# Fused attention, Sinkhorn gate and experts on one core: the first expert's weight loads put behind the transposes of five steps

## The chip, the cores and the metric

The kernel runs on one core of a Trainium2 chip. The metric is device time in microseconds (us). TensorE (PE) multiplies, VectorE (DVE) and ScalarE (ACT) work on tiles element by element, GpSimd (POOL) copies, and SyncE (SP) issues every DMA of this kernel from one queue.

## What is computed

The reference is attention with a bias learnt from relative positions, and behind it eight experts whose outputs are summed with weights from a Sinkhorn gate:

```python
def _attn_ref(q, k, v, w1, b1, w2):          # q, k, v: (4, 8, 576, 64)
    scores = scale * np.matmul(q, k.transpose(0, 1, 3, 2))
    ...
    h = np.maximum(x @ w1 + b1, 0.0)
    bias = h @ w2
    scores = scores + bias.transpose(2, 0, 1)[None, :, :, :]
    attn = np.exp(scores - np.max(scores, axis=-1, keepdims=True))
    attn = attn / (np.sum(attn, axis=-1, keepdims=True) + 1e-09)
    return np.matmul(attn, v)

def _moe_ref(x, w_gate, w1, w2):             # x: (2304, 512), 8 experts, F = 1024
    P = np.exp(logits - logits.max())        # then 8 Sinkhorn rounds on P
    for e in range(E):
        h = np.maximum(x @ w1[e], 0.0)
        out += P[:, e:e + 1] * (h @ w2[e])
```

Matrix products run as sums of three fp16 products: each fp32 operand is cut into a high and a low fp16 part.

## The kernel before

The kernel has two stages, each with a plan of its own. In the first, code records its instructions as nodes of a `Plan` (`record`, `node`), with the tile regions that each reads and writes; `Plan.emit` then runs a model of the engines with estimated durations and emits all nodes in the order in which the model starts them. So the order of every engine's instructions, and of SP's queue, comes from that model, and a dependency between nodes in the plan moves other nodes too. Waits between engines in the built program come from the tiles that instructions really touch. The plan holds SP's DMAs as an engine named "dma".

The attention part of stage one goes in steps (`steps`, `for n in range(NS + LAG + 1)`). A step treats one or two tiles of 128 queries of one head: PE makes scores `s`, DVE adds the bias and takes the minimum (`sb`), ACT takes the exponential, DVE the reciprocal (`st`), ACT and DVE write the high and low halves of the weights (`ah`, two buffers), and SP issues a DMA transpose of `ah` into `aT` (three buffers; `aT4` for single tiles). Two steps later PE multiplies `aT` with the values (`pv`), and the result goes to the expert input `xa`, `xb` or `xc`. Each unit of four tile pairs also loads `nat` (queries and keys), `vnat` (values) and `bt` (bias).

Beside the steps, `w_stage(j)`, called in step n = j + 6, brings in the weights of the first expert: `w_load(which, i)` issues one load of 512 KB (which = 0 is layer 1, which = 1 is layer 2, four loads each) into a part of `area`; `w_max` takes the largest absolute value of a load (a reduction on DVE, for two of the loads an activation on ACT); `w_scale` makes the scale of a layer from them; `w_cut` cuts a load into two fp16 halves (ACT and DVE). The places of the layer-1 loads 2 and 3 were used by the bias before, whose last results SP moves from `area` to `br`; those loads wait for these transfers. `e0_pieces` are pieces of expert 0's matmuls on PE (`l` tiles), put between the steps once weights and inputs are there.

The call that the change rewrites stands at L1061 to L1067 of the kernel before:

```python
if j == 0:
    for i in (2, 3):
        w_load(0, i)
    for i in (2, 3):
        w_max(0, i)
    for i in range(4):
        w_load(1, i)
```

Stage two (from the gate matmuls at L1264 on) computes the gate and all experts with a plan of its own.

Of the kernel before, what the change touches and what calls it, by code (L numbers as in the profile page):

```python
# [42 lines left out]
class Plan:  # L43
# [11 lines left out]
        ("pe", "dve"): 0.2,  # L55
    }

    def record(self, eng, cost, fn, ins, outs, move=None):
        g = self.group
        if g is not None:  # L60
            g[0] = eng
            g[1] += cost
            g[2].append(fn)
            for new, l in ((ins, g[3]), (outs, g[4])):
                l.extend(r for r in map(region, new) if r not in l)
            return
        self.node(eng, cost, fn, [region(x) for x in ins], [region(x) for x in outs], move)
# [40 lines left out]
        self.node(g[0], g[1], lambda: [f() for f in g[2]], g[3], g[4])  # L108

    def __init__(self):  # L110
        self.group, self.seen, self.prio = None, {}, 1
        self.nodes, self.writer, self.readers = [], {}, {}

    def add(self, eng, cost, fn, reads=(), writes=(), prio=1, after=0.0):
# [59 lines left out]
def region(ap):  # L174

    b = mybir.dt.size(ap.dtype)
    dims, off = list(ap.ap), ap.offset
    p = (0, 1)
    if ap.space != DRAM:
        step, n = dims.pop(0)  # L180
        p = (off // step, off // step + n)
        off %= step
    lo, hi = off * b, (off + sum((n - 1) * st for st, n in dims) + 1) * b
    if ap.space == PSUM:
        lo, hi = lo // 2048 * 2048, -(-hi // 2048) * 2048
    return ap.name, p, (lo, hi)
# [84 lines left out]
def attention_sinkhorn_moe(ctx, tc, q, k, v, w1, b1, w2, wg, m1, m2, xm, xm4, xf, sel, out):  # L271
# [11 lines left out]
    plan = Plan()  # L283
# [13 lines left out]
    def sm(shape):  # L297
        used[0] += shape[1]
        assert used[0] <= SMALL
        return sms[: shape[0], used[0] - shape[1] : used[0]]  # L300
# [100 lines left out]
    def w_src(e, which, i):  # L401
        if which == 0:
            return m1[e, i * P : (i + 1) * P, :]
        return m2[e, 2 * i * P : (2 * i + 2) * P, :].rearrange("(a p) d -> p a d", p=P)

    def w_dst(which, t):
        return t if which == 0 else t.rearrange("p (a d) -> p a d", a=2)
# [5 lines left out]
    with ExitStack() as actx:  # L413
# [375 lines left out]
        for n in range(8):  # L789
            for m in (2 * n, 2 * n + 1):  # L790
                nm, _, i = qk_order[m]
# [22 lines left out]
        g = sm([P, 1])  # L814
# [204 lines left out]
        def w_load(which, i):  # L1019
            raw[which, i] = f = wp[4 * which + i + 1]  # L1020
            sync.dma_start(out=w_dst(which, f), in_=w_src(0, which, i))

        def w_max(which, i):
            m, f = mw[:, 4 * which + i], raw[which, i]
            if (which, i) not in W_SUMS:
                absmax(m[:, 0:1], f)
                return
            for j in range(2):
                junk = wrk.tile([P, DM], F32, name="ys", tag="ys")
                act.activation(junk, f[:, 512 * j : 512 * j + 512], AF.Abs, accum_out=m[:, j : j + 1])  # L1030

        def w_scale(which):
            n = 2 - which
            m = sm([P, n])
            vec.tensor_reduce(
                out=m[:, 0:1], in_=mw[:, 4 * which : 4 * which + 4].rearrange("p n i -> p (n i)"), axis=AX.X, op=ALU.max
            )
            if which == 0:
                absmax(m[:, 1:2], wgt.rearrange("p a e -> p (a e)"))
            with plan.urgent():  # L1040
                u_, s_ = pow2(bcast_max(ps_small, m, n), n, TM14, TINY)
            wsc[which] = (u_[:, 0:1], s_[:, 0:1])
            if which == 0:
                wsc["ug"] = u_[:, 1:2]
                split(wgs[:, 0], wgs[:, 1], wgt, s_[:, 1:2])
            else:
                uw[0] = (wsc[0][0], wsc[1][0])

        def w_cut(which, i):
            w = wp[4 * which + i].bitcast(F16).rearrange("p (a n) -> p a n", a=2)  # L1050
            f, sc = raw.pop((which, i)), wsc[which][1]
            asplit(w[:, 0, :], w[:, 1, :], f, sc)
            (w1t if which == 0 else w2t).setdefault(0, {})[i] = w

        def w_stage(j):
            if j == -4:
                sync.dma_start(out=wgt, in_=wg.rearrange("(a p) e -> p a e", p=P))
            if j in (-4, -3):
                w_load(0, j + 4)
                w_max(0, j + 4)  # L1060
            if j == 0:  # L1061
                for i in (2, 3):
                    w_load(0, i)
                for i in (2, 3):
                    w_max(0, i)
                for i in range(4):
                    w_load(1, i)  # L1067
            if j == 5:
                w_scale(0)
                for i in range(4):  # L1070
                    w_cut(0, i)
            if j == 6:
                for i in range(4):
                    w_max(1, i)
                w_scale(1)
                for i in range(4):
                    w_cut(1, i)
# [7 lines left out]
        steps = []  # L1085
# [44 lines left out]
        W0 = 6  # L1130
        for n in range(NS + LAG + 1):
# [31 lines left out]
            if n == W0 - 1:  # L1163
                assert bpos[0] > NBLK
                hpl = Places(lambda k, n, size: area[:, 8192:])
            w_stage(n - W0)
            for _ in range(2 if n % 5 in (0, 2, 4) or n < 20 else 1):
                if pieces and n >= 13:
# [694 lines left out]
    for n, (e, b) in enumerate(seq):  # L1863
        r = visit[n]
        i, at_end, leaves = (b, r % 2), n % 5 == 4, visit[n + 1 : n + 2] != [r]
# [96 lines left out]
```

## Time and profile before

| what | us |
|---|---|
| median of 3 runs | 1778.55 |
| lowest and highest run | 1778.25, 1781.21 |
| profiled execution, its own time | 1782.07 |
| span of the profiled execution, first to last instruction | 1780.3 |
| PE, DVE, ACT busy in the span | 1682.0, 1448.0, 1087.9 |

The span is 1.8 us shorter than the time of the same execution; the rest lies around the instructions. The profiled execution took 3.5 us more than the median. Attention fills the span up to about 512 us, the gate and the rest of expert 0 some 70 us more, and the other experts what follows. All instructions of stage one are recorded by a helper and so carry its line, L210 (L217 in the changed kernel); they are told apart by their tiles.

### The profile page before, as it was taken

Reading aid. Unit: us, or ns where it says so; the run is one execution under the profiler, and the core shown is the slowest. Engines: PE = TensorE matmul, PEld = TensorE weight load, DVE = VectorE, ACT = ScalarE, POOL = GpSimd, SP = SyncE. Lnnn points to the kernel's source line nnn. Section 1 sums busy time; section 2 is a strip of 40 time slices with the busy share of each in tenths; the row PEclk is TensorE's granted clock in tenths of the full one; section 3 lists DMA queues with packets and bytes.
Section 4 is the critical chain, followed back from the end, with each engine's and each line's share of the span. In section 5 each row is a group of like instructions: output and inputs, shape, how many; then the busy total and the mean of one; then the engine's idle time right before and its main releaser. Section 6 shows DMA issues by size and latency. Waiting matters only on the chain.

```text
span 1780.3 us, 40365 instructions
## 1 busy us (share of the span) xinstructions
PE 1682.0 (94%) x16640; PEld 1374.5 (77%) x16640; DVE 1448.0 (81%) x2627; ACT 1087.9 (61%) x1930; POOL 79.9 (4%) x91
## 2 busy tenths in 40 slices
PE   7886897899989999999999999999999999999998
PEld 4554564555666788888988898889888988898887
DVE  6987989889967898778878787878788878876666
ACT  7886888788855675645564555564555544453443
POOL 0120112212200000000000000000000000000000
PEclk9988899999989999999999999999999999999999
DMA  7769999999893254645474556445655653463321
GB/s 256 246 160 223 207 210 204 188 205 194 190 281 117 85 197 179 231 156 173 170 276 135 196 198 241 155 149 212 209 177 179 240 187 131 163 237 102 104 73 36
DMA packets 294141, 323.70 MB, mean 182 GB/s; under 512 B 184252, under 2 KB 220612, under 8 KB 288964
## 3 DMA queue, kind: packets, MB, share of 16 engines
q1 hardware_dynamic: 293956, 321.12, 60.6%
q8 instruction: 130, 2.13, 0.5%
q14 instruction: 55, 0.45, 0.1%
HBM read 189.33 MB, written 88.08 MB: 156 GB/s over the span
## 4 chain that ended last, share of the span: by engine, by line
PE 83%; DVE 6%; DMA 5%; ACT 3%; issue 2%; SPq 0%; DVEq 0%; ACTq 0%
PE bankA L1585 18%; PE bankA L1605 14%; PE bankE L1585 9%; PE bankE L1605 9%; PE bankB L1605 9%; PE l L210 7%; PE bankB L1585 5%; PE s L210 4%; PE pv L210 3%; DMA aT<-ah 3%; ACT area L210 2%; PE bankA L393 2%; DVE area L210 1%; DVE ah L210 1%; DVE sb L210 1%
## 5 line engine op out<-in xcount | busy, mean ns | idle before, releaser
L1585 PEld LDWEIGHTS <-slot 128*128 128x128 f16 x5040 | 450.7, 98 | 49.9 <-issue 4.1
L1605 PEld LDWEIGHTS <-hA 128*128 128x128 f16 x2268 | 222.3, 98 | 27.3 <-issue 0.6
L210 PEld LDWEIGHTS <-area 128*128 128x128 f16 (+1 forms) x2477 | 153.6, 100 | 102.7 <-issue 35.0
L1585 PE MATMUL bankA<-xt,slot 128*128 128x256 f16 (+1 forms) x1680 | 186.1, 262 | 1.8 <-ACT u L1642 1.8
L1585 PE MATMUL bankE<-xt,slot 128*128 128x256 f16 (+1 forms) x1680 | 186.1, 262 | 0.0
L1630 ACT ACTIVATE hA<-c 128x512 f16<-128x512 f32 x189 | 118.2, 627 | 110.0 <-DVE c L1208 109.1
L1605 PEld LDWEIGHTS <-hS 128*128 128x128 f16 x1512 | 147.3, 98 | 21.7 <-ACT hS L1630 2.8
L1605 PEld LDWEIGHTS <-area 128*128 128x128 f16 x1512 | 147.9, 98 | 18.5 <-issue 1.4
L1208 DVE SCALAR_TENSOR_TENSOR hA<-c,hA 128x512 f16<-128x512 f32 x189 | 127.6, 686 | 14.2 <-ACT hA L1630 12.2
L210 DVE SCALAR_TENSOR_TENSOR ah<-sb,st,ah 128x576 f16<-128x576 f32 x144 | 120.6, 863 | 18.6 <-ACT ah L210 18.4
L1689 ACT COPY u<-bankA 128x512 f32<-128x512 f32 (+1 forms) x70 | 37.9, 542 | 158.8 <-PE bankA L1605 158.4
L210 ACT ACTIVATE ah<-sb,st 128x576 f16<-128x576 f32 x144 | 106.4, 772 | 34.2 <-DMA aT<-ah 29.6
L1642 ACT ACTIVATE u<-bankA 128x512 f32<-128x512 f32 x126 | 75.2, 597 | 68.1 <-PE bankA L1585 63.9
L210 PE MATMUL l<-area 128*128 128x512 f16 (+1 forms) x413 | 110.8, 385 | 4.9 <-ACT area L210 1.5
L210 ACT ACTIVATE sb<-sb,st 128x576 f32<-128x576 f32 x144 | 110.5, 769 | 7.9 <-DVE st L210 7.4
L1208 DVE SCALAR_TENSOR_TENSOR acc<-c,fs,acc 128x256 f32<-128x256 f32 x252 | 110.7, 481 | 2.0
L210 PE MATMUL s<-qkT 128*128 128x512 f16 (+3 forms) x560 | 83.5, 301 | 21.9 <-DVE st L210 21.0
L1605 PE MATMUL bankA<-area,hS 128*128 128x256 f16 x756 | 88.6, 273 | 2.9 <-ACT hS L1630 2.2
L1605 PE MATMUL bankA<-area,hA 128*128 128x256 f16 x756 | 89.9, 276 | 0.0
L1605 PE MATMUL bankA<-area 128*128 128x256 f16 x756 | 88.2, 273 | 1.0 <-ACT u L1689 1.0
L1605 PE MATMUL bankE<-area,hS 128*128 128x256 f16 x756 | 88.3, 273 | 0.0
L1605 PE MATMUL bankB<-area,hA 128*128 128x256 f16 x756 | 88.2, 273 | 0.0
(240 smaller groups left out, 3155.0 us busy)
## 6 DMA issues: line engine op xcount, KB each, us to landing
sc_w<-stage SPq DMA_DIRECT2D x84, 512.0 KB
acc<-sc_y SPq DMA_DIRECT2D x102, 256.0 KB
area<-sc_w SPq DMA_DIRECT2D x48, 512.0 KB
sc_y<-acc SPq DMA_DIRECT2D x84, 256.0 KB
xt<-sc_t SPq DMA_DIRECT2D x18, 1024.0 KB
slot<-sc_w SPq DMA_DIRECT2D x36, 512.0 KB
bt<-sc_bias SPq DMA_DIRECT2D x26, 576.0 KB
raw<-in_moe_w_dram SPq DMA_DIRECT2D x28, 512.0 KB
```

Of the source, the lines that this page charges most:

```text
L210: self.plan.record(self.name, cost, lambda: fn(*args, **kw), ins, outs, move)
L393: pe.matmul(ps[:, :512], h[a][:, ft, j * P : (j + 1) * P], w[:, wl, c : c + 512], start=(ft == 0 and i == 0), stop=(ft == 7 and i == 2),)
L1208: vec.scalar_tensor_tensor(out=o, in0=x, scalar=s, in1=y, op0=op0, op1=op1)
L1585: pe.matmul(ps[:, jf * w : jf * w + w], t[:, a, c * 512 + f * P : c * 512 + f * P + P], x(xp, c), start=(first and jf == 0 and c == 0 and ...
L1605: pe.matmul(ps[:, j * 256 : j * 256 + 256], h[:, a, fc * w + j * P : fc * w + j * P + P], t[:, wp, fc * 256 : fc * 256 + 256], start=(firs ...
L1630: on_act(0.58, lambda: act.activation(h[:, 0, sl], x, AF.Relu if relu else AF.Copy), [r], wk)
L1642: on_act(0.55, lambda: act.activation(tmp[k], bank[b], f, scale=HS), [b], [k], 0)
L1689: on_act(0.27 * nt, lambda: act.copy(tmp[k][:, :n], bank[b][:, :n]), [b], [k], 0)
```

## The change

`Plan` gets a context manager `behind`: while it is open, each recorded node also counts the given tiles as inputs. With it the loads of `w_stage` are put behind the transpose of a step, in the plan alone:

```diff
+    @contextmanager
+    def behind(self, *aps):
+
+        self.also = list(aps)
+        yield
+        self.also = []
+
     def record(self, eng, cost, fn, ins, outs, move=None):
-        g = self.group
+        g, ins = self.group, [*ins, *self.also]
...
-            if j == 0:
-                for i in (2, 3):
-                    w_load(0, i)
+            if 0 <= j < 5:
+                with plan.behind(steps[j + W0 - 1]["aT"]):
+                    for i in (2, 3) if j == 0 else (j - 1,):
+                        w_load(int(j > 0), i)
+            if j == 2:
                 for i in (2, 3):
                     w_max(0, i)
-                for i in range(4):
-                    w_load(1, i)
```

(`W0` is 6, the first step behind the bias.) The layer-1 loads 2 and 3 stay in step 6, the four layer-2 loads go to steps 7 to 10, and the reductions of the layer-1 loads 2 and 3 are recorded in step 8. The numbers of instructions of PE, ACT and POOL stay the same, and so do those of the loads.

SP's queue from the last two value loads before the weight loads on, in the kernel before (`moe_w` are the weight loads; 128x1024 is layer 1, 128x2x512 layer 2; x2 is two in a row):

```order
L210 DMA vnat_116<-in_v_dram 64x2x256
L210 DMA area<-in_moe_w_dram 128x2x512
L210 DMA br_111<-area 64x4x128 x2
L210 DMA_TRANSPOSE aT_123<-ah_144 128x18x128
L210 DMA br_111<-area 64x4x32 x2
L210 DMA area<-in_moe_w_dram 128x1024
L210 DMA br_111<-area 64x4x32 x2
L210 DMA area<-in_moe_w_dram 128x2x512 x2
L210 DMA area<-in_moe_w_dram 128x1024
L210 DMA area<-in_moe_w_dram 128x2x512
L210 DMA_TRANSPOSE aT_125<-ah_142 128x18x128
L210 DMA_TRANSPOSE aT_138<-ah_144 128x18x128
```

The first weight load stood ahead of the transpose into aT_123, and five stood between that one and the next two. From here on the same place in the changed kernel, up to the second layer-2 load:

```order
L217 DMA_TRANSPOSE aT_123<-ah_144 128x18x128
L217 DMA br_111<-area 64x4x128 x2
L217 DMA nat_128<-in_k_dram 128x576
L217 DMA nat_120<-in_q_dram 128x576
L217 DMA br_111<-area 64x4x32 x2
L217 DMA area<-in_moe_w_dram 128x1024
L217 DMA br_111<-area 64x4x32 x2
L217 DMA_TRANSPOSE aT_125<-ah_142 128x18x128
L217 DMA area<-in_moe_w_dram 128x1024
L217 DMA_TRANSPOSE aT_138<-ah_144 128x18x128
L217 DMA area<-in_moe_w_dram 128x2x512
L217 DMA bt_122<-sc_bias 128x1152
```

The transpose into aT_123 now comes first, one layer-1 load stands before that into aT_125 and one behind it, and two `nat` loads have moved in ahead of them. Behind these rows the queue goes on so:

```order
L217 DMA area<-in_moe_w_dram 128x2x512
L217 DMA_TRANSPOSE aT_123<-ah_142 128x18x128
L217 DMA bt_124<-sc_bias 128x1152
L217 DMA area<-in_moe_w_dram 128x2x512
L217 DMA_TRANSPOSE aT_125<-ah_144 128x18x128
L217 DMA_TRANSPOSE aT_0_118<-ah_142 128x9x128
L217 DMA bt_122<-sc_bias 128x1152
L217 DMA area<-in_moe_w_dram 128x2x512
L217 DMA_TRANSPOSE aT_138<-ah_144 128x18x128
```

The layer-2 loads stand between the next transposes, the second one directly behind a `bt` load. On DVE, before, the reductions of the loads (`TENSOR_REDUCE sms<-area`) stood together:

```order
L210 TENSOR_REDUCE sms<-area 128x1
L210 TENSOR_SCALAR st_132<-st_132 128x1
L210 RECIPROCAL st_132<-st_132 128x1
L210 TENSOR_REDUCE sms<-area 128x1 x2
L210 TENSOR_REDUCE sms<-sms 128x1
L210 TENSOR_REDUCE sms<-l_0_114 2x1
L210 TENSOR_SCALAR sms<-ident,sms 2x2
L210 TENSOR_REDUCE sms<-area 128x1
```

Now two of them stand between the cuts of layer 1 (`area<-area`) and the work of the steps (`ISA sb` adds the bias and takes the minimum), and the two others further on:

```order
L217 SCALAR_TENSOR_TENSOR area<-area,sms 128x1024
L217 TENSOR_REDUCE sms<-area 128x1
L217 TENSOR_SCALAR st_135<-st_135 128x2
L217 TENSOR_REDUCE sms<-area 128x1
L217 SCALAR_TENSOR_TENSOR ah_142<-sb_136,st_132,ah_142 128x576
L217 SCALAR_TENSOR_TENSOR area<-area,sms 128x1024
L217 ISA sb_141,st_139<-s_117,bt_124,sms 128x576
```

The work of the steps that stood behind all reductions now stands among them. The order of all engines differs from here to the end of the attention part, in patches that grow smaller.

## Rows read from the trace of the kernel before

**Rows 1.** The page: the chain that ended last, by engine.
```profile
PE 83%; DVE 6%; DMA 5%; ACT 3%; issue 2%; SPq 0%; DVEq 0%; ACTq 0%
```

**Rows 2.** Timeline of PE (start us, us, engine, line, operation): the first gate matmuls.
```profile
512.46 1.36 PE L1264 MATMUL bankS<-wgs,xa 128*128 128x8 f16 x48
```

**Rows 3.** Busy time by stretch: length, each engine's us (instructions), clock, DMA share, GB/s.
```profile
core 0: us, PE busy (x) PEld busy (x) DVE busy (x) ACT busy (x) POOL busy (x), PEclk, DMA share, GB/s
150.00:160.00 10.00, 5.85 (x62) 3.28 (x59) 9.96 (x24) 7.33 (x16) 0.00 (x0) 0.98 1.11 258
160.00:190.00 30.00, 17.30 (x102) 9.21 (x101) 22.85 (x56) 15.46 (x31) 0.00 (x0) 0.56 1.01 232
190.00:210.00 20.00, 16.03 (x164) 10.68 (x164) 19.62 (x40) 19.13 (x33) 1.63 (x3) 0.91 0.96 230
210.00:250.00 40.00, 39.21 (x408) 25.40 (x409) 36.83 (x83) 33.12 (x68) 7.58 (x7) 1.00 0.94 182
250.00:300.00 50.00, 42.53 (x411) 26.52 (x410) 44.90 (x98) 42.23 (x86) 9.29 (x10) 0.93 1.02 215
```

**Rows 4.** The chain of waits, 165 to 186 us: start us, us, what.
```profile
165.39 3.00 DMA br<-area
...
168.54 0.86 DMA area<-in_moe_w_dram
169.40 8.70 DMA aT<-ah
178.13 1.44 ACT ah L210 x2
...
185.65 2.09 PE s L210 x8
```

**Rows 5.** Timeline of SP's queue, 154 to 179 us.
```profile
154.01 0.53 SPq L210 DMA_DIRECT2D area<-in_moe_w_dram  x1
...
157.16 5.12 SPq L210 DMA_TRANSPOSE aT<-ah  x1
...
164.16 0.54 SPq L210 DMA_DIRECT2D area<-in_moe_w_dram  x1
...
166.05 3.31 SPq L210 DMA_DIRECT2D area<-in_moe_w_dram  x4
169.40 9.55 SPq L210 DMA_TRANSPOSE aT<-ah  x2
```

**Rows 6.** Timelines of DVE (two rows of `ah`, one reduction) and ACT.
```profile
159.71 0.82 DVE L210 SCALAR_TENSOR_TENSOR ah<-sb,st,ah 128x576 f16<-128x576 f32 x1
...
165.31 1.55 DVE L210 SCALAR_TENSOR_TENSOR ah<-sb,st,ah 128x576 f16<-128x576 f32 x2 [1.96 <-ACT ah L210]
...
172.10 1.22 DVE L210 TENSOR_REDUCE sms<-area 128x1 f32<-128x1024 f32 x1 [2.13 <-DMA area<-in_moe_w_dram]
...
178.13 1.44 ACT L210 ACTIVATE ah<-sb,st 128x576 f16<-128x576 f32 x2 [6.94 <-DMA aT<-ah]
```

**Rows 7.** Timeline of SP's queue, 194 to 201 us.
```profile
194.84 0.42 SPq L210 DMA_DIRECT2D nat<-in_k_dram  x1
196.17 3.62 SPq L210 DMA_TRANSPOSE aT<-ah  x1
...
200.47 0.42 SPq L210 DMA_DIRECT2D nat<-in_q_dram  x1
```

**Rows 8.** DMA engines, 40 slices: 150:160, 160:180 (and GB/s), 180:200, 250:270, 270:290.
```profile
DMA  9986899999977798999999999999999999999999
...
DMA  9932999553768998998989569999998699999999
GB/s 141 66 52 33 227 290 291 126 66 65 82 139 328 396 215 114 242 221 266 336 332 283 180 242 328 340 410 395 332 247 166 101 291 289 286 240 216 219 217 212
...
DMA  9399999999995299999959931199099669999999
...
DMA  9897049999999996999999940599299991999994
...
DMA  7840049999009998989999919998797999999994
```

**Rows 9.** Groups by form, 150 to 300 us: count, busy us, mean ns, idle before.
```profile
L210 DVE TENSOR_REDUCE sms<-area 128x1 f32<-128x1024 f32 x5 | 6.1, 1213 | 2.2 <-DMA area<-in_moe_w_dram 2.1
```

**Rows 10.** The chain of waits at 230 us.
```profile
230.06 1.08 PE s L210 x8
```

More of the change, by code (lines that the diff above doesn't have):

```diff
@@ L110, in __init__ @@
     def __init__(self):
-        self.group, self.seen, self.prio = None, {}, 1
+        self.group, self.seen, self.prio, self.also = None, {}, 1, []
         self.nodes, self.writer, self.readers = [], {}, {}
```

## The prediction

> **What bounds the kernel now.** The chain that ended last is 83% PE over the whole span [rows 1], but the change touches only the attention stage, which ends where the gate matmuls start at 512.46 us [rows 2]; behind that the instruction streams stand in the same order as before. So I read the stretch around the weight loads: first busy time by stretch, then the chain, then SP's queue. In 150 to 160 us DVE is busy 9.96 of 10 us; in 160 to 190 us it is busy 22.85 of 30 us, PE gets a clock of 0.56 and ACT does 15.46; from 190 us on DVE (19.62 of 20) and then PE (39.21 of 40 in 210 to 250 us) are nearly full again [rows 3]. The hole of 160 to 190 us is 7.15 us of DVE time. The chain says what fills it: 3.00 us of SP waiting until `br` transfers land, 0.86 us for a load, then 8.70 us of a transpose, then ACT's `ah` [rows 4]. SP's queue shows why: the weight loads start at 154.01, 164.16 and 166.05 us (four in a row, 3.31 us), and the two transposes behind them are issued at 169.40 us [rows 5]. The first of them was ready when its `ah` was written, at 159.71 + 0.82 = 160.53 us [rows 6]: it stood 8.9 us in SP's queue and 8.70 us more in the rings. ACT then waited 6.94 us, and DVE 2.13 us for a load [rows 6].
>
> **The change part by part.** Nothing is computed less; 6 loads of 512 KB, 5 reductions and 8 cuts move. In the built program a load gets no wait on the transpose of its step; what holds it back is its place in SP's queue.
>
> (a) Out of the way of two transposes. Data in the stretch of the stall moves at 232 GB/s [rows 3], so a load of 512 KB is 0.524 MB / 232 = 2.26 us. The transpose issued at 157.16 us loses the load of 154.01 us in front of it: 2.3 us. The one issued at 169.40 us had five loads between itself and the transpose before (2.62 MB, 11.3 us); now it has one load and the two `nat` loads of 288 KB each, which the planner pulls forward from 194.84 us and about 200 us [rows 5, 7] into the gap: 1.11 MB, 4.8 us. That is 6.5 us less, with (2.3) up to 8.8 us. Taken as useful: no more than DVE's hole, 7.15 us.
>
> (b) Given back. The other five loads (one of layer 1, four of layer 2) now stand between the next transposes, each paying 2.26 us in the rings, 11.3 us until the transpose that was issued at 196.17 us. By then the queue has moved what it moved before, and one `nat` load more (0.29 MB, 1.3 us, which is missing later). So what is won at that point can only be idle time of the DMA engines in 150 to 200 us. Count the slices of [rows 8], a 9 as full and any other digit d as d/10 + 0.05: idle 0.39 us in 150 to 160, 2.72 us in 160 to 180, 3.15 us in 180 to 200, together 6.3 of 50 us, 43.7 us of work. If the same work packs as densely as in 150 to 160 us (4% idle), it takes 43.7 / 0.96 = 45.5 us: 4.5 us won; with the extra `nat` load 45.0 / 0.96 = 46.9 us: 3.1 us won. Why so dense: after a transpose lands, ACT and DVE need 1.44 + 1.55 us for the next `ah` [rows 6], and a load of 2.26 us in the queue fills just that gap. If it packs as in 250 to 290 us (7.0 of 40 us idle, 17.5%) [rows 8], nothing is won and up to 3 us lost. I take the middle of 3.1 and 4.5, 3.8 us, since a queue that always holds a load is nearest to the row of 150 to 160 us.
>
> (c) DVE's reductions and cuts. Before, four reductions of 1.21 us fell into the hole, where DVE had nothing else; now they stand among the attention steps (four `w_max` rows spread over 27 rows of DVE's list). 4 x 1.21 = 4.9 us [rows 9] must find room where DVE is 98% busy until 210 us, then 92% and 90%: the idle there is 0.38 + 3.17 + 5.10 = 8.65 us until 300 us [rows 3]. Their cost lies between 0 (all in that idle time) and 4.9 us; I take 0, because the chain from 210 us on is PE's, not DVE's, and keep the other end for the range. The 8 cuts keep their cost; the last comes three `ah` writes later, but PE's first expert pieces need only layer 1's four.
>
> (d) PE's clock. In 160 to 190 us it is 0.56, mostly the lower level of 1.2 GHz; eight score matmuls on the chain took 2.09 us there and 1.08 us at 230 us [rows 4, 10]. If the hole closes and the clock stays up, 1.0 us comes on top; from below 0. Taken: 0.
>
> Sum: 3.8 us off the attention stage. Later stages keep their durations: 1782.07 - 3.8 = 1778.3 us for the profiled execution, which lay 3.5 us above the median of the runs; for the median, 1778.55 - 3.8 = **1774.8 us** (0.21%).
>
> The first transpose also shows the rule on which (a) rests: five loads of 2.26 us from 164.16 us on, and then a transpose of 0.59 MB at the 216 GB/s of the slices around 179 us [rows 8], 2.7 us, give 178.2 us; it landed at 169.40 + 8.70 = 178.10 us [rows 4]. The Trainium skill states this in "DMA: Bandwidth & Descriptors", section "Queues, rings and completion order": each DMA engine takes the descriptors of SP's ring in ring order. Here the trace agrees. The same rule speaks against the change: spreading moves no byte off the ring, so a transpose late by a load stays late by a load. That is the first rival.
>
> **The rivals.** *The same bytes in one ring.* What the first two transposes win, the next five pay, and the idle share of the DMA engines stays at 12.6% as it is: 43.7 / 0.874 = 50 us. Then 1778.5 us. For it: DMA is at 232 to 258 GB/s there, more than the 182 to 215 of later stretches [rows 3]; against it: the idle slices lie just around the late transposes (161 to 166 us, 191 to 196 us) [rows 8]. Chance 0.33. To it belongs the case that the change does not do what it says: two layer-2 loads and a `bt` load stand ahead of one transpose (aT_123 in the new order), and the `nat` loads take the freed place.
>
> *DVE waits for the loads one by one.* DVE runs in order. A reduction that reaches its load before it has landed holds up the score minimum and the `ah` behind it, as the row with 2.13 us shows [rows 6]. Before, this happened once, in a hole; now four reductions stand between steps, and each of their loads can be held up by the transpose ahead of it in the ring. Four such waits are 8.5 us; less the 3.8 us won, 4.7 us slower: 1783.3 us. It decides from the second wait of that size. For it: the loads are now issued just in time; against it: SP's queue puts each load ahead of the transpose whose `ah` DVE needs anyway. Chance 0.2.
>
> *The rest of the order.* The planner reorders all engines until 512 us (the new order returns to the old only in patches). Between equal orders of this kind I have no row; the DMA rows bound it at 3 us either way. It widens the range and moves no centre.
>
> **How the numbers follow.** Forecast 0.47 (1771 to 1776.5 us by itself), same bytes 0.33, DVE waits 0.20. This kernel's measurement can tell about 0.2%, 3.6 us, from no change: faster means under 1775.0 us, slower over 1782.1 us. The forecast lies only 0.2 us beyond the first bound, so of its 0.47 I count 0.34 as faster and 0.13 as same. Of the second case 0.22 is same, 0.08 faster and 0.03 slower by reordering; of the third 0.13 slower, 0.07 same. Together 0.42 faster, 0.42 same, 0.16 slower. The range: below, DVE's whole hole and PE's clock, 7.15 + 1.0 us, and 1 us of reordering, 1769.4; above, the DVE rival at 1783.3 us.
>
> **What would show it.** Right: no transpose in 150 to 200 us that takes over 6 us to land, ACT's longest wait on `aT` under 4 us, DVE busy over 26 of 30 us in 160 to 190 us, and the gate matmuls starting near 508.7 us. (a) wrong: the transpose behind the `nat` loads still lands after 175 us. (b) wrong: DMA idle in 150 to 200 us stays at 6 us or more. (c) wrong: reductions in DVE's list with idle time put down to the loads, over 2 us each. The whole is wrong if the gate matmuls start where they did although the stall is gone: then it was given back between 200 and 300 us.

## The result and the profile after

| | before | after |
|---|---|---|
| median of the runs of this comparison, us | 1780.19 | 1794.18 |
| lowest and highest, us | 1778.25, 1786.6 | 1789.53, 1796.81 |
| profiled execution, own time and span, us | 1782.07, 1780.3 | 1796.81, 1795.0 |
| first gate matmul, us | 512.46 | 524.58 |

The changed kernel is slower: the ratio is 1.0066, with an interval of 1.0044 to 1.0088, some 12 us. The forecast was 1774.8 us, its range ended at 1783.3. Nearly all of it is there when the gate starts [rows 2]; the row that answers to it, from the timeline of PE after:

```profile
524.58 1.36 PE L1271 MATMUL bankS<-wgs,xa 128*128 128x8 f16 x48
```

Busy time by stretch after, columns as in [rows 3]:

```profile
160.00:190.00 30.00, 13.96 (x95) 7.64 (x94) 22.59 (x51) 17.79 (x34) 0.00 (x0) 0.67 1.03 240
190.00:210.00 20.00, 15.90 (x142) 10.23 (x142) 16.72 (x41) 13.50 (x26) 1.61 (x3) 0.76 0.86 212
210.00:250.00 40.00, 33.54 (x350) 21.14 (x348) 36.69 (x73) 32.89 (x63) 7.45 (x7) 0.90 0.73 158
```

DVE's hole in 160 to 190 us did not close: 22.59 us busy, 22.85 before. From 190 us on, where DVE and then PE had been nearly full, there are gaps: DVE is busy 16.72 us in 190 to 210 us (19.62 before), and PE does 33.54 us of work in 210 to 250 us where it did 39.21.

The stall itself is gone. SP's queue and the longest wait of ACT for a transpose in 150 to 200 us, after, beside [rows 5, 6]:

```profile
167.86 3.69 SPq L217 DMA_TRANSPOSE aT<-ah  x1
...
172.59 3.59 SPq L217 DMA_TRANSPOSE aT<-ah  x1
176.23 0.57 SPq L217 DMA_DIRECT2D area<-in_moe_w_dram  x1
176.85 0.46 SPq L217 DMA_DIRECT2D bt<-sc_bias  x1
177.35 0.43 SPq L217 DMA_DIRECT2D area<-in_moe_w_dram  x1
177.88 6.21 SPq L217 DMA_TRANSPOSE aT<-ah  x1
184.13 0.57 SPq L217 DMA_DIRECT2D bt<-sc_bias  x1
...
192.20 0.44 SPq L217 DMA_DIRECT2D area<-in_moe_w_dram  x1
...
177.94 1.44 ACT L217 ACTIVATE ah<-sb,st 128x576 f16<-128x576 f32 x2 [1.90 <-DMA aT<-ah]
```

ACT's wait is 1.90 us where it was 6.94. The last layer-2 load is issued at 192.20 us; before, all four were out by 169.4 us [rows 5].

To see where time is won and lost, add up PE's matmul durations in order (each shape at its median over the kernel before) and ask how much later the changed kernel reaches the same sum. That "lag", worked out so from the matmul records of each profiled execution:

| lag behind before's profile, us, at | 150 | 185 | 195 | 215 | 225 | 250 | gate |
|---|---|---|---|---|---|---|---|
| after | 3.7 | -0.1 | 4.7 | 10.5 | 9.4 | 11.0 | 12.1 |

If the shapes are weighted by their columns instead, single values here and below move by up to 1.5 us (10.8 instead of 9.4 us at 225 us), so only steps of several us are read from them. At 150 us the two kernels have run the same instructions, so the 3.7 us there are spread between executions, and the trace accounts for 8.4 of the 12.1 us. From 150 us on, 3.8 us are won until 185 us, 4.8 lost until 195 us, 5.8 lost until 215 us, then nearly nothing. Behind the gate there is only spread: over all kernels below, the end of the span differs from that of the kernel before by -3.7 to +2.7 us more than the gate does.

What stands in the loss from 195 to 215 us, in timelines of DVE, ACT and PE. Before:

```profile
207.05 1.28 DVE L210 SCALAR_TENSOR_TENSOR area<-area,sms 128x1024 f16<-128x1024 f32 x1
208.37 1.07 ACT L210 CAST area<-l 128x512 f16<-128x512 f32 x2
209.84 1.28 DVE L210 TENSOR_TENSOR area<-l,area 128x512 f16<-128x512 f32 x2
210.57 1.47 PE L210 MATMUL l<-xa,area 128*128 128x256 f16 x12 [0.85 <-DVE area L210]
```

After:

```profile
201.86 1.21 DVE L217 TENSOR_REDUCE sms<-area 128x1 f32<-128x1024 f32 x1
205.39 0.28 DVE L217 TENSOR_REDUCE sms<-l 1x1 f32<-1x128 f32 x1 [1.11 <-PE l L217]
208.72 1.28 DVE L217 SCALAR_TENSOR_TENSOR area<-area,sms 128x1024 f16<-128x1024 f32 x1
218.04 1.27 DVE L217 SCALAR_TENSOR_TENSOR area<-area,sms 128x1024 f16<-128x1024 f32 x1
219.35 1.07 ACT L217 CAST area<-l 128x512 f16<-128x512 f32 x2 [0.48 <-DVE area L217]
220.89 1.28 DVE L217 TENSOR_TENSOR area<-l,area 128x512 f16<-128x512 f32 x2
221.03 1.17 PE L217 MATMUL s<-xc 128*64 128x512 f16 x8 [2.82 <-DVE st L217]
222.13 2.70 PE L217 MATMUL l<-xa,area 128*128 128x256 f16 x12
```

The chain is the same in both: the last cut of layer 2, then ACT's copy of the first hidden results of expert 0 (`area<-l`, the CAST), DVE's low half, PE's next expert piece. After, it starts 11 us later, because the reduction of the last load (201.86 us) comes late, and with it the scale and all four cuts. Why a hidden result waits for a cut of layer 2 is in the places: the raw load 3 of layer 2 lies in `area[:, 8192:9216]`, and the hidden tile `h` of expert 0 in `area[:, 8192:10240]`. PE has two PSUM tiles for these pieces; with four pieces in them it can go on only when `h` takes them. PE's row of the fifth piece (222.13 us) shows no idle time of its own: the planner, which knows the places, has put it behind score and value matmuls, and PE's idle time stands ahead of those, some 8 us in 205 to 222 us (2.2 us in the kernel before), 2.82 of them in the row at 221.03 us.

### The profile page after: what moved, and what is told of

It is laid out like the page before. It is cut to its first block, busy times and chain, and to the rows that moved or that the text cites. A ratio compares the mean times of both kernels' runs of the same rounds, so it can differ in the third digit from the quotient of the medians.

```text
span 1795.0 us, 40366 instructions
## 1 busy us (share of the span) xinstructions
PE 1686.1 (94%) x16640; PEld 1376.2 (77%) x16640; DVE 1447.1 (81%) x2627; ACT 1086.9 (61%) x1930; POOL 80.3 (4%) x91
## 4 chain that ended last, share of the span: by engine, by line
PE 80%; DVE 9%; DMA 5%; ACT 3%; issue 3%; SPq 0%; DVEq 0%; ACTq 0%
PE bankA L1592 18%; PE bankA L1612 13%; PE bankE L1592 9%; PE bankE L1612 9%; PE bankB L1612 9%; PE l L217 8%; PE s L217 4%; PE bankB L1592 4%; PE pv L217 3%; DMA aT<-ah 2%; ACT area L217 2%; DVE sb L217 2%; DVE ah L217 1%; DVE area L217 1%; DVE sms L217 1%
## 5 line engine op out<-in xcount | busy, mean ns | idle before, releaser
L1215 DVE SCALAR_TENSOR_TENSOR hA<-c,hA 128x512 f16<-128x512 f32 x189 | 127.4, 685 | 12.7 <-ACT hA L1637 10.5
L1612 PE MATMUL bankE<-area,hA 128*128 128x256 f16 x756 | 88.3, 273 | 0.0
```

Source lines behind the costliest of these rows:

```text
L1215: vec.scalar_tensor_tensor(out=o, in0=x, scalar=s, in1=y, op0=op0, op1=op1)
L1612: pe.matmul(ps[:, j * 256 : j * 256 + 256], h[:, a, fc * w + j * P : fc * w + j * P + P], t[:, wp, fc * 256 : fc * 256 + 256], start=(firs ...
```

## Experiments

Each kernel is one edit of the kernel before or of the changed one. "Fixed order" means that the planner's result is kept and single rows are moved in the emitted list, so that all other rows stand as they were. Ratios are to the kernel before; the changed kernel is 1.0066.

### Loads moved back alone, and DVE's reductions priced

My first theory after the result was DVE's list: reductions and cuts that had fallen into the hole now stand ahead of the score minima. In the changed kernel, fixed order, the six loads go back in SP's queue, as far as it allows (`last`, a load's inputs, can hold one behind its old place):

```diff
+            spots = [seq.index(turns[5])] + [seq.index(turns[6])] * 5
...
+                put.append((max(spots[k], last), k, i))
+            for p, k, i in sorted(put, reverse=True):
+                seq.insert(p, i)
```

> PE, DVE, ACT and POOL keep the changed kernel's order word for word; in SP's queue alone six weight loads go back in front of the transposes where the kernel before had them. Theory (the order on DVE costs the time): the reductions and cuts still stand ahead of the score minimum, and the stall comes back on top of them: 1794 to 1800 us. Rival (the loads hold up the later transposes): the loss goes with the loads, 1784 us or less.

Measured: 1799.05 us, 1.0093 (1.0078 to 1.0108). The loads' new place by itself seems to help: with it the kernel is some 4.8 us faster (0.27%, though the intervals overlap) than with the same order and the loads put back. Here SP's queue and ACT:

```profile
165.75 0.41 SPq L238 DMA_DIRECT2D area<-in_moe_w_dram  x1
...
169.83 3.10 SPq L238 DMA_DIRECT2D area<-in_moe_w_dram  x5
172.98 9.84 SPq L238 DMA_TRANSPOSE aT<-ah  x2
...
182.17 1.44 ACT L238 ACTIVATE ah<-sb,st 128x576 f16<-128x576 f32 x2 [5.68 <-DMA aT<-ah]
```

The stall of [rows 4] is back, ACT's `ah` comes at 182.17 us and not at 177.94. The queue is not quite the old one: the first load went not ahead of the transpose issued at 157.25 us but behind it (165.75 us), and the two `nat` loads stayed, so six loads and two `nat` stand ahead of the two late transposes where five loads stood. Counted from the lag at 150 us, the first of these two is back some 1 us later than in the kernel before, so the 4.8 us are, if anything, a little too much. (The Trainium skill, "DMA: Bandwidth & Descriptors", section "Queues, rings and completion order", has each DMA engine take SP's descriptors in ring order; the rows at 169.83 and 172.98 us agree with it.) The loss is in the order of the engines or in what the order stands for.

The reductions, in both kernels with the order kept:

```diff
-                absmax(m[:, 0:1], f)
+                if (which, i) == (0, 0):
+                    absmax(m[:, 0:1], f)
+                    return
...
+                    lambda: nc.vector.tensor_reduce(
+                        out=m[:, 0:1], in_=f[:, :8], axis=AX.X, op=ALU.max, apply_absolute_value=True
+                    ),
...
```

> The changed kernel in its own order, with five of the weights' reductions on DVE made short: each takes its maximum over the first 8 of 1024 columns, the rest is left out. DVE does 5 x 1.1 = 5.5 us less. Theory (the reductions stand where DVE is full): 5 to 8 us less than the changed kernel, 1786 to 1789 us. Rival (PE's new order of scores and expert pieces alone costs the time): within 2 us of the changed kernel, 1792 to 1796 us.

> The kernel before in its own order, with the same five reductions made short (maximum over the first 8 of 1024 columns). Theory: they lay in DVE's hole and cost nothing there, so the time stays: 1778 to 1781 us. Rival (a reduction costs its 1.2 us wherever it stands): 4 to 6 us less, 1774 to 1776 us.

Measured: 1.0040 (1.0025 to 1.0055) and 0.9986 (0.9975 to 0.9997). The reductions cost the changed kernel 4.6 us and the kernel before 2.5 us, so they explain about 2 us of the 12, which is less than the intervals can tell from nothing. The chain of the last cut is unchanged: the lag still rises from 0.4 us at 205 to 7.2 us at 215 us. Then four maxima go to ACT:

```diff
-W_SUMS = ((0, 1), (0, 3))
+W_SUMS = ((0, 1), (0, 3), (1, 0), (1, 1), (1, 2), (1, 3))
```

> The changed kernel with the four layer-2 maxima taken by ACT (activations with a sum, as for two layer-1 loads) and not by DVE; the planner orders anew. ACT was busy 17.8 of 30 us in 160 to 190 us. Theory (DVE is short of time): 1784 to 1790 us. Rival (PE's order, or the loads in the ring): 1792 us or more, since neither changes much; it would also be that if ACT took DVE's place as the late engine.

Measured: 1792.52 us, 1.0063 (1.0049 to 1.0076). As the rival had it. But ACT takes the last maximum no earlier (its second half starts at 200.99 us), and the last cut starts at 218.1 us, as late as before this edit. So less DVE work alone doesn't bring the time back; as the planner orders this kernel anew, the run by itself doesn't rule DVE out.

### The place of the hidden tile

So I looked for what PE's fifth piece waits for, and came to the chain shown above. The halves of the first hidden tile change places, so that its first four results lie in `area[:, 9216:10240]`, off the raw load:

```diff
+                    if first:
+                        h = h.rearrange("p a f n -> p (a f n)").rearrange("p (g a f n) -> p g a f n", g=2, a=2, f=4)
...
+                    box["out"] = (lambda ft: (ft % 4, h[:, 1 - ft // 4])) if first else (lambda ft: (ft, h))
```

> The changed kernel; the halves of the first hidden tile of expert 0 change places, so that its first four results no longer lie where the raw load 3 of layer 2 lies until it is cut. New theory: the last layer-2 load comes late, its cut (218.0 us) frees that place, and PE's expert pieces from the fifth on wait for it, 205 to 222 us: 4 to 7 us less than the changed kernel, 1787 to 1790 us. Rival (DVE has too much work there, whatever waits): within 2 us of the changed kernel, 1792 to 1796 us.

> The same exchange of places in the kernel before. There the last cut came at 207.05 us and PE idled only 0.85 us ahead of its fifth piece. New theory: 0 to 2 us less, 1778 to 1781 us. Rival (the exchange helps by another order of all engines, not by that wait): as much less as in the changed kernel, 1774 to 1776 us.

Measured: 1784.43 us, 1.0022 (1.0009 to 1.0034), and 1782.74 us, 1.0006 (0.9995 to 1.0017). The exchange takes 0.44%, some 8 us, off the changed kernel (3 to 12 us by the two intervals; the two traces differ by 4.0 us between 150 us and the gate) and nothing off the kernel before. There too the fifth piece comes earlier, at 205.70 and not at 210.57 us, but PE had other work and idled only 0.85 us ahead of it. Since the planner knows the places, it orders both kernels anew from about 200 us on. In the changed kernel with it (ACT, PE, DVE, ACT, PE):

```profile
200.99 0.57 ACT L217 CAST area<-l 128x512 f16<-128x512 f32 x1
...
202.96 1.47 PE L217 MATMUL l<-xa,area 128*128 128x256 f16 x12
...
216.69 1.27 DVE L217 SCALAR_TENSOR_TENSOR area<-area,sms 128x1024 f16<-128x1024 f32 x1
218.08 0.58 ACT L217 CAST area<-l 128x512 f16<-128x512 f32 x1
...
219.67 1.17 PE L217 MATMUL s<-xc 128*64 128x512 f16 x8 [2.04 <-DVE st L217]
```

The fifth piece starts at 202.96 us, 19 us earlier. The last cut is as late as before the edit (216.69 us), and the later half of the hidden tile still waits for it (the CAST at 218.08 us): the lag jumps from -0.8 us at 215 to 4.9 us at 225 us. So the exchange defers that wait, it does not end it.

### The 5 us between 185 and 195 us

There PE waits 6.03 us for DVE to free a score tile (after, PE):

```profile
191.72 1.17 PE L217 MATMUL s<-qkT 128*64 128x512 f16 x8 [6.03 <-DVE st L217]
```

Fixed order, two score minima pulled in front of two reductions, an `ah` and a cut; then the same with the exchange:

```diff
+            late = [i for i in seq[at:] if self.tag.get(i) == "sb"][:2]
...
+            seq[at:at] = late
```

> The changed kernel in its own order but for two rows on DVE: the two score minima that ran at 190.84 and 191.58 us go in front of two reductions, one `ah` row and one cut (at 186.60 us). New theory: PE's 6.03 us of idle time at 191.72 us was the wait for these two rows; 3 to 5 us less than the changed kernel, 1789 to 1791 us. Rival (DVE is full, so what is put first delays the rest): within 2 us, 1792 to 1796 us.

> Both edits together. New theory: the two waits add up, 1782 to 1786 us, 8 to 12 us less than the changed kernel; what the freed transposes won (about 4 us) might show below the kernel before only if nothing else was lost. Rival (DVE full): 1790 us or more.

Measured: 1.0089 (1.0074 to 1.0104) and 1.0038 (1.0025 to 1.0052): worse, not better. DVE in the first of them shows why:

```profile
187.87 0.82 DVE L231 CUSTOM_DVE_ANT_0 sb<-s,bt,sms 128x576 f32<-128x576 f32 x1 [2.34 <-DMA bt<-sc_bias]
```

The minima reach a bias load that hasn't landed: in the changed queue the second `bt` is issued at 184.13 us, behind a layer-2 load and a transpose, where the kernel before issued two in a row (179.00 us). So both `bt` loads go in front of the layer-2 loads, alone and with the other moves:

```diff
+            two = [i for i in seq[at:] if self.tag.get(i) == "bt"][:2]
...
+            for i in two:
...
+                seq.insert(at, i)
```

> The changed kernel in its own order but for SP's queue: two bias loads (`bt`), which stood behind the first and the second layer-2 load and a transpose (issued at 176.85 and 184.13 us), go in front of these loads, both in a row as in the kernel before (179.00 us, two). Theory (PE's 6.03 us of idle time before 191.72 us begins with the second bias load): the score minima still stand behind reductions and a cut on DVE, so only 0 to 2 us less than the changed kernel, 1792 to 1794 us. Rival (the weight loads' own place in the ring decides): nothing, 1794 us; if the bias alone was it: 1789 to 1791 us.

> A repeat of the same kernel for a second profile of the stretch 176 to 200 us, beside the timed one: the same numbers as for it.

> The changed kernel with both small moves: the two bias loads in front of the layer-2 loads in SP's queue, and the two score minima in front of two reductions, an `ah` row and a cut on DVE. Theory (the wait before 191.72 us needed both, since with one alone the minima waited for the other): PE's 6 us of idle time falls to some 2, and 3 to 5 us go: 1789 to 1791 us. Rival (DVE is full, and the 8 us of expert pieces that wait later swallow what is won): within 2 us of the changed kernel, 1792 to 1796 us.

> The changed kernel with the exchanged hidden halves and both small moves. Theory: all three losses found are mended, the freed transposes' 4 us remain: 1777 to 1781 us, at or a little under the kernel before. Rival (what is first delays the rest on a full DVE): as with the exchange alone, 1783 to 1788 us.

Measured: 1793.14 us, 1.0070 (1.0053 to 1.0086), with 1791.42 us in the repeat; both moves 1793.48 us, 1.0067 (1.0055 to 1.0079); with the exchange 1786.65 us, 1.0029 (1.0017 to 1.0041). The wait goes, the time doesn't. PE with both moves:

```profile
185.22 1.17 PE L243 MATMUL s<-qkT 128*64 128x512 f16 x8 [1.78 <-DVE st L243]
...
190.21 0.28 PE L243 MATMUL l<-xa,area 128*128 128x256 f16 x1 [1.57 <-DVE area L243]
191.44 0.61 PE L243 MATMUL l<-xa,area 128*128 128x256 f16 x2 [0.95 <-ACT area L243]
```

The scores come 6.5 us earlier (1.7 of it by the lag at 150 us), and PE then stands in its first expert piece, which needs layer 1's cuts; the last two of these start at 188.9 and 191.4 us (189.65 and 192.32 us in the changed kernel), behind reductions and now also behind the two score minima. That the scores would bring 3 to 5 us was wrong.

All edits together, with the short reductions of above:

> The changed kernel with the exchanged hidden halves, both small moves and the five reductions made short (maximum over the first 8 of 1024 columns, the rest is left out). Theory (around 190 us the score minima, the bias load, the cuts and the reductions each hold PE up as soon as the others don't): with the reductions gone as well nothing is left that was lost, and the 4 us of the freed transposes show: 1776 to 1780 us. Rival (PE's own order, 5 us in 185 to 195 us, remains): 1783 to 1786 us.

Measured: 1785.26 us, 1.0024 (1.0012 to 1.0035), no better than the exchange alone. The gain of the theory did not come. The lag, from 4.8 us at 150 us, is 1.2 us at 215 us and 6.0 us at 225 us: until 215 us the kernel is 3.6 us ahead of where it started, and then the wait for the last cut (218.73 us there) takes it back.

### When the last load comes

What is left is the time of the last layer-2 load. Four at once in step 7 (shown), two and two in steps 7 and 8, and all six behind the transpose of step 6:

```diff
-            if 0 <= j < 5:
+            if j in (0, 1):
                 with plan.behind(steps[j + W0 - 1]["aT"]):
-                    for i in (2, 3) if j == 0 else (j - 1,):
+                    for i in (2, 3) if j == 0 else range(4):
```

> The changed kernel with the four layer-2 loads not one to a step but all behind the transpose of step 7; the planner orders anew. Theory (what counts is when the last layer-2 load comes, since its cut frees the place of the hidden tile): most of the 8 us goes, 1780 to 1786 us. Rival (the place of the loads in the ring between transposes): four loads in a row hold up one transpose by 9 us, 1786 us or more.

> The same with two layer-2 loads in step 7 and two in step 8. Theory: between that kernel and the changed one by the time of the last load, 1783 to 1790 us. Rival (the ring): nearer to the kernel before than with four in a row.

> All six loads behind the transpose of step 6; DVE's reductions and cuts then stand nearly as in the kernel before. Theory: the last cut is as early as before and the first transpose loses the load in front of it (2.3 us): 1776 to 1781 us. Rival (every new order costs a few us by chance): 1783 to 1788 us.

Measured: 1791.29 us, 1.0062 (1.0048 to 1.0076); 1786.22 us, 1.0035 (1.0024 to 1.0046); 1781.56 us, 1.0002 (0.9993 to 1.0011). The second is as expected, the last 0.6 us above what was expected. The first is not: four loads in a row in front of a transpose brought the old stall back at another step, as the rival said. SP's queue and PE there:

```profile
174.04 2.11 SPq L217 DMA_DIRECT2D area<-in_moe_w_dram  x4
176.19 0.69 SPq L217 DMA_DIRECT2D bt<-sc_bias  x1
176.99 6.75 SPq L217 DMA_TRANSPOSE aT<-ah  x1
...
216.47 1.87 PE L217 MATMUL l<-xa,area 128*128 128x256 f16 x8 [3.33 <-DVE area L217]
```

Its lag rises by 5.5 us between 180 and 185 us, and by 4.3 us more between 210 and 215 us. Here PE waits 3.33 us right ahead of its fifth piece, for DVE's low half of the hidden tile, which follows the last cut (213.08 us). That cut is late although the last load is out by 176.2 us: its maximum is taken by 190.41 us, but the scale goes through PE only at 197.51 us, behind score and value matmuls, the scores among them having waited for DVE. With two and two, the last load is out by 177.5 us and the last cut starts at 212.69 us. So the time of the last load isn't all that sets the last cut.

Then the kernel before with one load moved to where the change puts it (against the kernel before; `behind` is left out):

```diff
+                for i in range(3):
+                    w_load(1, i)
+            if j == 4:
+                with plan.behind(steps[j + W0 - 1]["aT"]):
+                    w_load(1, 3)
+            if j == 2:
                 for i in (2, 3):
                     w_max(0, i)
-                for i in range(4):
-                    w_load(1, i)
```

> The kernel before with one load alone moved: layer 2's load 3 goes behind the transpose of step 10, where the change puts it; the five others and all recorded reductions stay. One load less (2.3 us) stands ahead of the two late transposes. Theory (the last load alone makes the scale, the four cuts and the hidden tile late): 4 to 10 us more than the kernel before, 1785 to 1791 us, with a wait of PE ahead of its fifth expert piece. Rival (the loss came from all six loads' new places): within 2 us of the kernel before, 1779 to 1783 us.

Measured: 1790.82 us, 1.0057 (1.0043 to 1.0072). One load of eight, late, costs 10 us. (The edit also records the reductions of the layer-1 loads 2 and 3 in step 8, as the change does, so "all recorded reductions stay" is not so. But DVE's order is that of the kernel before up to the late load's own reduction, and the kernel with all six loads behind step 6, which has the same lines, lies at 1.0002.) Its path (SP, DVE, ACT, PE):

```profile
188.14 0.44 SPq L217 DMA_DIRECT2D area<-in_moe_w_dram  x1
...
194.89 1.22 DVE L217 TENSOR_REDUCE sms<-area 128x1 f32<-128x1024 f32 x1
...
199.82 0.28 DVE L217 TENSOR_REDUCE sms<-l 1x1 f32<-1x128 f32 x1 [2.19 <-PE l L217]
...
204.95 1.28 DVE L217 SCALAR_TENSOR_TENSOR area<-area,sms 128x1024 f16<-128x1024 f32 x1
...
213.83 1.27 DVE L217 SCALAR_TENSOR_TENSOR area<-area,sms 128x1024 f16<-128x1024 f32 x1
...
215.14 1.07 ACT L217 CAST area<-l 128x512 f16<-128x512 f32 x2 [0.25 <-DVE area L217]
...
216.63 1.28 DVE L217 TENSOR_TENSOR area<-l,area 128x512 f16<-128x512 f32 x2
...
217.37 2.72 PE L217 MATMUL l<-xa,area 128*128 128x256 f16 x12 [0.17 <-DVE area L217]
```

From the issue to the first cut are 16.8 us, to the freed place 27 us: reduction, a scale that goes through PE behind expert pieces, four cuts that take turns with the work of the steps. The lag is 7.1 us at 250 us and 10.2 us from 390 us on; what costs these last 3 us the path doesn't show.

> The kernel with two layer-2 loads in step 7 and two in step 8, and the hidden halves exchanged. Theory: the 6 us that it lost between 210 and 215 us are the wait for the last cut; without it 1778 to 1782 us, the kernel before's time or a little under it. Rival: 1784 us or more, as without the exchange.

Measured: 1787.93 us, 1.0042 (1.0029 to 1.0056), no gain: the theory's number was wrong. With the exchange the lag no longer rises between 205 and 215 us (6.1, then 6.0 us), but the 6 us wait for the score tile stays (6.25 us at 196.12 us), and 3.1 us are lost between 260 and 280 us, half of them regained by 300 us. So the wait behind the last cut can go without the time going; why is open. No version of the spread loads got under the kernel before.

The lags of the runs that carry the argument:

| lag, us, at | 150 | 185 | 195 | 215 | 225 | 250 | gate |
|---|---|---|---|---|---|---|---|
| loads back | 2.9 | 7.9 | 11.6 | 17.0 | 15.9 | 17.5 | 18.5 |
| changed, exchanged halves | 1.2 | -2.3 | 2.5 | -0.8 | 4.9 | 4.6 | 5.6 |
| before, last load late | -0.7 | -1.5 | 0.4 | 6.0 | 4.9 | 7.1 | 10.7 |
| all six behind step 6 | 1.9 | 1.8 | 2.3 | 3.0 | 3.5 | 3.6 | 1.7 |

## Why the prediction was wrong, point by point

**(a) Two transposes freed.** Right for one of the two. ACT's longest wait fell to 1.90 us (the text asked for under 4), and the transpose behind the `nat` loads was in by 172.95 us (the chain has it from 167.86 us for 5.09 us). The first gained nothing. PE's value matmuls that wait for it, before and after:

```profile
164.44 3.42 PE L210 MATMUL pv<-aT,xb 128*64 128x256 f16 x27 [3.11 <-DMA aT<-ah]
...
165.36 3.43 PE L217 MATMUL pv<-aT,xb 128*64 128x256 f16 x27 [3.17 <-DMA aT<-ah]
```

Issued at 157.16 us before and at 157.94 us after, it took some 7.3 and 7.4 us, with a weight load ahead of it and without. The 2.3 us of this term did not come: that load had been issued 3.15 us ahead of the transpose [rows 5], and other transfers stand ahead of it now. The sign that no transpose takes over 6 us failed here, and also for the one behind two layer-2 loads and a `bt` load, whose issue alone kept SP's queue for 6.21 us (177.88 us).

**(b) What of it is kept.** The size fits as far as it was measured, and the reason was wrong, so the fit is partly luck. PE's work is 3.8 us further at 185 us, and the loads' place alone is worth about 4.8 us, with intervals that overlap; I took 3.8. But the DMA engines did not pack more densely: counted as in the prediction, their slices of 150 to 200 us after leave 6.4 us idle, 6.3 before [rows 8]. That sign spoke for the first rival, and the gain came all the same, in a ring that is as full as it was, with the one long wait of ACT gone (6.94 us before, 1.90 after).

```profile
DMA  9823799899294799988899999999899999676999
...
DMA  8992799999978797998996999497799999959999
...
DMA  9765999999958967999999999998989960005999
```

(150 to 160, 160 to 180 and 180 to 200 us after; the empty slices near 197 us are the queue waiting for an `ah`.)

**(c) Reductions and cuts.** Here the prediction broke. It priced them as DVE time, 0 to 4.9 us, took 0 because the chain is PE's, and put the cuts aside with "the last comes three `ah` writes later, but PE's first expert pieces need only layer 1's four". The inputs of these pieces need only those; the place of their results needs the last cut of layer 2. The reductions as DVE time are worth about 2 us of the difference, within the intervals. That one load, late, gives 10 us in the kernel before, where the change as a whole costs 12, and the exchange of places takes some 8 us back in the changed one. The sign named for (c), idle time of DVE ahead of the reductions, looked at the wrong engine: there was none.

**(d) The clock.** In 160 to 190 us it was 0.67 (0.56 before), in 190 to 210 us 0.76 (0.91 before): a mix of the two levels of 1.2 and 2.4 GHz that moved to the later stretch together with PE's idle time (6.03 us ahead of 191.72 us). What it costs by itself was not measured: twelve matmuls of an expert piece took 2.75 us at 193.77 us and 1.48 us at 199.26 us after, and 2.74 us at 197.30 us before.

**The rivals.** *The same bytes in one ring*: right on idle time and on the later transposes behind loads (6.21 us at 177.88 us), not on the one behind the `nat` loads. *DVE waits for the loads one by one*: it ended on the right side by luck, through another mechanism. The five reductions had no idle time in front of them (2.2 us before [rows 9]):

```profile
L217 DVE TENSOR_REDUCE sms<-area 128x1 f32<-128x1024 f32 x5 | 6.0, 1212 | 0.0
```

*The rest of the order* I bounded at 3 us either way by DMA rows, which say nothing of it; with the loads put back, the changed order cost 16 to 17 us, the late cut among it. That bound and the 0 of (c) made the range too short.

**What stays open.** The 5 us between 185 and 195 us of the changed kernel. Three waits were taken away there one by one and together, and the time stayed: the next row in line was late each time. Whether it is one cause or just four engines in an order that fits other times isn't settled. Nor is it why the exchange gains 8 us with the loads in five steps and nothing with the loads two and two.

## What to carry to other kernels

Before a load is moved to a later step, follow its place as well as its data: who uses that memory next, and who waits for that user; here PE waited for a tile that shared its place with the last raw load. Where one scale is made of several loads, nothing behind the scale can start before the last of them, so one load that comes late enough makes all of it late (with the last load at 188.14 us, the first cut came at 204.95 us). When a planner makes the order, keep its result and move single rows in it: that told the loads' place (a gain of about 5 us, with intervals that overlap) from all that came with the order (a loss of 16 to 17 us), which the two kernels alone show only as a sum.

## What the runs showed of the hardware that was not expected

Kernels with the same instructions up to 150 us reached the same PE work there with lags between -0.7 and 5.2 us. One profiled execution is that far from another before anything differs, so two traces are to be compared by how a lag changes, not by its value.
